# A fused attention and feed-forward kernel: issuing one ScalarE step of the weight preparation one tick later during the first matrix product

## The chip, the core and the metric

The kernel runs on one core of one Trainium2 chip. The metric is the device time of one launch in microseconds (us); lower is better. The core has five engines that run on their own instruction queues, each strictly in order: TensorE (PE) multiplies matrices, VectorE (DVE), ScalarE (ACT) and GpSimd (POOL) work on elements, and SyncE (SP) here only issues DMA transfers. They wait for one another through semaphores.

## The reference

```python
def _attn_ref(q, k, v, g_q, g_k):            # q, k, v: (8, 12, 448, 64) float32
    q_n, k_n = (rmsnorm(q, g_q), rmsnorm(k, g_k))
    scores = np.matmul(q_n, k_n.transpose(0, 1, 3, 2)) / np.sqrt(64)
    attn = softmax(scores)
    return np.matmul(attn, v)

x = attn_out.transpose(0, 2, 1, 3).reshape(3584, 768)
h = x @ w_in                                  # w_in: (768, 2048) float64
g = np.maximum(h, 0.0) ** 2
out = g @ w_out                               # w_out: (2048, 768) float64
```

## The kernel before

**Stages.** The eight batches are taken in four spans of two batches (896 tokens). Span 0 begins with its attention alone. Then comes its first matrix product, called L1 here: `x @ w_in`, relu, square. After that each span's second product (`g @ w_out`) runs interleaved with the next span's attention, and each later span's first product follows. The change concerns L1 of span 0 only, roughly 133 to 261 us of the profiled execution.

**Seven products for eight.** Each matrix product is done by a Strassen-Winograd scheme: a two-by-two block product is made of seven block products, A11, S2, S1, S3, A12, A22 and S4, whose left sides are quadrants of the weights or sums of quadrants. L1 has eight columns of blocks, f = 0 to 7, of seven block products each. Number these products u = 0 to 55, so that u = 7f + position. Within a column the order is A11, S2, S1, S3, A12, A22, S4 (in column 0: A11, S1, A12, S2, S3, S4, A22). Each product is three 128x128 blocks against 448 columns; the trace shows it as six matmuls.

**What follows a product.** The results are collected in PSUM (TensorE's output memory):

- A11: ACT copies it out (`p1`, L1102).
- S2: DVE adds `z = p1 + pb` (L1106).
- S1: DVE adds `y = z + pc` (L1109).
- S3, A22, S4: DVE adds the product to `y` or `z` (L1114), then ACT takes the relu (L1066) and the square (L1068) of the sum.
- A12: ACT takes relu and square straight from PSUM.

Products share banks: `pb`, `pc` and `pd` alternate between two banks. So S3 may start only when S2's add has been made, the next column's S2 only when this column's S4 add has been made, and A22 (which accumulates onto S3's bank) only when S3's add has been made. Each of these three adds has the length of one product, about 2.25 us, between the end of its own product and the start of the product that needs the bank.

**Preparing the weights.** The weights come as float64. Thirty-two chunks n = 0 to 31 (128 partitions x 768 values; 0 to 15 from `w_in`, 16 to 31 from `w_out`) are turned into float32 on the chip, while attention and L1 run. The generator `prepare(t)` does this in four ticks for each t:

- tick 1: SP stores the finished seven blocks of an earlier pair of chunks to DRAM (L598, odd chunks n = t-3 only); DVE clamps the high words of chunk t (L603). The clamp reads what `unsigned(t)` wrote.
- tick 2: ACT scales the low words (L606); DVE shifts bits into a PSUM scratch (L608).
- tick 3: DVE merges sign and bits (L613); DVE adds the parts of chunk t-1 to its float32 value (L579).
- tick 4: POOL forms the sums S1 to S4 for odd chunks (L583; all four operations of a pair run once the chunk's value is there); SP starts loading later words (L543).

`unsigned(n)` is one ACT instruction: the absolute value of the high words of chunk n (Abs, L589, 128x768). It is called for chunk t+1 during `prepare(t)`, and the clamp of chunk t+1 in the next tick waits for it.

**Which tick comes after which product.** The loop over L1 (L1502 to L1507) yields after each product and then runs ticks up to number `min(ALL, EARLY + (ALL - EARLY) * (u - 1) // (N1 - 6))`, that is min(140, 52 + 88(u-1)//50); tick s of chunk t has number 4t + s. So between one and two ticks follow each product. The order of instructions within each engine's queue is the order in which this code emits them; nothing reorders them. Chunks t < 13 are prepared during attention (EARLY // 4 = 13), the rest in L1.

**Loads.** SP loads each weight block (`sw`, five buffers, L672) into the buffer that the product five places earlier has left; the stores of L598 stand in the same queue and wait for POOL's sums.

Of the kernel before, what the change touches and what calls it, by code (L numbers as in the profile page):

```python
# [387 lines left out]
def attention_then_ffn_bounded(  # L388
# [100 lines left out]
    EARLY, ALL = 4 * 13, 4 * (2 * NFC + 3)  # L489
# [9 lines left out]
    def pairs_of(words):  # L499
        both = words.rearrange("p (n two) -> p n two", two=2)  # L500
        return both[:, :, 0], both[:, :, 1]

    def words_of(n):
        place = n % WORDS
        if place == 0:
            at = BLOCKS * 8 * HW + EXPS * NW
            flat = stage[:, at:at + 2 * NW]
        elif place < 3:
            f = (NFC, HF)[place - 1] - 2
            flat = gT[:, f:f + 2, :].rearrange("p f n -> p (f n)")[:, 0:2 * NW]  # L510
        else:
            if (n, "words") not in spare:
                spare[n, "words"] = spare["pool"].tile([P, 2 * NW], F32, tag="words", name="words", bufs=WORDS - 3)
            flat = spare[n, "words"]
        return flat.bitcast(U32)

    def blocks_of(n):
        at = n // 2 % BLOCKS * 8 * HW
        return stage[:, at:at + 8 * HW].rearrange("p (k m) -> p k m", k=8)

    def place_of(n, k):

        return 7 * int(n >= NFC) if k == A21 else k + int(n < NFC)

    def exponents_of(n):
        at = BLOCKS * 8 * HW + n % EXPS * NW
        return stage[:, at:at + NW]
# [17 lines left out]
    def load_words(t, done):  # L545

        while loaded[0] <= t + WORDS - 3 and loaded[0] < max(done, 0) + WORDS:
            load_w(loaded[0])
            loaded[0] += 1

    def prepare(t):

        def there(n):
            return 0 <= n < 2 * NFC

        def parts(n):
            low, high = pairs_of(words_of(n))
            return exponents_of(n), exponents_of(n).bitcast(U32), low, high  # L560

        def value(n, half):
            if not there(n):
                return

            to = ((A11, A12), (A21, A22)) if n < NFC else ((A11, A21), (A12, A22))
            places = [place_of(n, k) for k in to[n % 2]]
            part = slice(half * HW, (half + 1) * HW)
            if not doubles:
                nc.gpsimd.tensor_copy(blocks_of(n)[:, places[half]], words_of(n).bitcast(F32)[:, part])  # L570
                return
            _, eu, low, _ = parts(n)
            if n < EARLY // 4:
                dst = blocks_of(n)[:, places[half]]
                nc.gpsimd.tensor_tensor(*[x.bitcast(I32) for x in (dst, low[:, part], eu[:, part])], ALU.add)
            elif half == 0:
                dst = blocks_of(n)[:, places[0]:places[1] + 1:places[1] - places[0]]
                low, eu = (x.rearrange("p (h m) -> p h m", h=2) for x in (low, eu))
                nc.vector.tensor_tensor(*[x.bitcast(I32) for x in (dst, low, eu)], ALU.add)  # L579

        def total(n, dst, x, y, op):
            if there(n) and n % 2:
                nc.gpsimd.tensor_tensor(*[blocks_of(n)[:, place_of(n, i)] for i in (dst, x, y)], op)  # L583

        def unsigned(n):

            if there(n) and doubles:
                e, _, _, high = parts(n)
                nc.scalar.activation(e, high.bitcast(F32), AF.Abs)  # L589

        if t == 0:
            unsigned(0)
        n = t - 3
        if there(n) and n % 2:
            c = n % NFC // 2
            dst = w1s[c] if n < NFC else w2s[:, c // 4, :, c % 4]
            first = place_of(n, A11)
            nc.sync.dma_start(dst.rearrange("k p m -> p k m"), blocks_of(n)[:, first:first + 7])  # L598
            written[0] = n + 1
        if there(t) and doubles:  # L600
            e, eu, low, high = parts(t)

            nc.vector.tensor_scalar(e, e, 2.0 ** -15, 1.875 * 2.0 ** 16, ALU.max, ALU.min)  # L603
        yield
        if there(t) and doubles:
            nc.scalar.activation(low.bitcast(I32), low, AF.Copy, scale=2.0 ** -29)  # L606
            bits = banks.get("bits", eu)
            nc.vector.tensor_scalar(bits, eu, 3, 0x3FFFFFF8, ALU.logical_shift_left, ALU.bitwise_and)  # L608
        if t < 3:
            load_words(t, t - 1)  # L610
        yield
        if there(t) and doubles:
            nc.vector.scalar_tensor_tensor(eu, high, 0xC0000000, bits, ALU.bitwise_and, ALU.bitwise_or)  # L613
        total(t - 2, S3, A11, A21, ALU.subtract)
        total(t - 2, S4, A12, S2, ALU.subtract)
        value(t - 1, 0)
        if t >= EARLY // 4:
            unsigned(t + 1)
        yield
        if t < EARLY // 4:  # L620
            unsigned(t + 1)
        value(t - 1, 1)
        total(t - 1, S1, A21, A22, ALU.add)
        total(t - 1, S2, S1, A11, ALU.subtract)
        load_words(t, t - 1)
        yield

    def ticks():
        for t in range(2 * NFC + 3):
            yield from prepare(t)  # L630
# [1009 lines left out]
```

## Time and profile before

| | |
|---|---|
| median of 3 runs | 1345.16 us (1345.02 to 1346.12) |
| the profiled execution's own time | 1345.02 us |
| its span, first to last instruction | 1343.1 us |
| TensorE busy | 1324.0 us (99% of the span) |
| VectorE busy | 860.5 us (64%) |
| ScalarE busy | 486.2 us (36%) |
| GpSimd busy | 681.1 us (51%) |
| mean granted TensorE clock | 0.998 |

The profiled execution lasts 1.9 us longer than its span; the difference lies before the first and after the last instruction. A row of the timeline gives the start, the duration, the engine, the line, what is written and read, and in brackets how long the engine had been idle and what released it. On DVE and ACT an instruction can start before the one ahead of it has quite ended, so the distance between two starts is what an instruction costs its queue. A row of the table by stretches gives for each engine its busy time and number of instructions, then the granted clock, the share of the DMA engines' time, and GB/s.

### The profile page before, as it was taken

To read this page: it belongs to the slowest core of one execution; us is meant where nothing else is said; L and a number is where in the kernel's file an instruction comes from. 1 tells how busy PE (TensorE), PEld (TensorE's weight loads), DVE (VectorE), ACT (ScalarE), POOL (GpSimd) and SP (SyncE) were. 2 spreads that over 40 slices of the span, in tenths; PEclk is the share of its full clock that TensorE was granted. 3 is DMA by queue.
4 is the path that set the end of the run, shared out by engine and by line. 5 is a ranking of instruction groups with operands and counts; after the bars stand their busy time and mean duration, and the time that the engine had idled before them with its cause. 6 is when DMAs were issued, how large, how long until landed. Compare 5 with 4: busy or idle time off the path is not lost.

```text
span 1343.1 us, 17769 instructions
## 1 busy us (share of the span) xinstructions
PE 1324.0 (99%) x5930; PEld 699.4 (52%) x5930; DVE 860.5 (64%) x1333; ACT 486.2 (36%) x939; POOL 681.1 (51%) x546
## 2 busy tenths in 40 slices
PE   8999999999999999999999999999999999999997
PEld 3333544444446655444444755444444665556887
DVE  6999888489988233467887523457878723336553
ACT  7886566455541012245543011235554101111000
POOL 5766534376765222647774522448676522322452
PEclk9999999999999999999999999999999999999999
DMA  8978899656664433356656432345664444431333
GB/s 225 240 221 218 289 372 307 213 124 132 133 148 119 102 88 88 97 116 125 145 127 144 109 91 88 95 114 115 134 130 124 120 92 143 128 88 47 115 104 55
DMA packets 413817, 190.18 MB, mean 142 GB/s; under 512 B 282388, under 2 KB 408724, under 8 KB 413716
## 3 DMA queue, kind: packets, MB, share of 16 engines
q1 hardware_dynamic: 406164, 180.21, 51.8%
q0 software_dynamic: 4736, 8.40, 2.4%
q8 instruction: 49, 0.80, 0.3%
q10 hardware_dynamic: 2816, 0.34, 0.2%
q14 instruction: 52, 0.43, 0.1%
HBM read 155.72 MB, written 33.16 MB: 141 GB/s over the span
## 4 chain that ended last, share of the span: by engine, by line
PE 86%; DVE 7%; ACT 3%; DMA 3%; issue 1%; POOL 0%; SPq 0%; DVEq 0%; ACTq 0%; POOLq 0%
PE ps L1198 21%; PE pd L1098 10%; PE pa L1098 10%; PE pc L1098 10%; PE sc L799 7%; PE pav L881 7%; PE pb L1098 5%; PE ps L1381 3%; PE ps L1249 2%; PE pd L1353 2%; PE pc L1353 2%; PE pa L1353 2%; PE pd L1183 1%; PE pc L1183 1%; DMA sw<-w1s 1%
## 5 line engine op out<-in xcount | busy, mean ns | idle before, releaser
L1070 POOL TENSOR_TENSOR gT<-gT 128x448 f32<-128x448 f32 x96 | 93.7, 978 | 258.5 <-ACT gT L1066 258.5
L764 POOL TENSOR_TENSOR half<-half,mhalf 128x28 f32<-128x28 f32 x36 | 185.2, 5145 | 69.5 <-DVE half L763 54.9
L1198 PE MATMUL ps<-gT,sw 128*128 128x448 f32 x432 | 169.3, 545 | 0.0
L1066 ACT ACTIVATE gT<-gT 128x448 f32<-128x448 f32 x96 | 55.4, 577 | 296.2 <-DVE gT L1114 296.2
L1098 PE MATMUL pa<-xT,sw 128*128 128x448 f32 x384 | 154.9, 539 | 0.5 <-DMA sw<-w1s 0.5
L1198 PEld LDWEIGHTS ps<-gT,sw 128*128 128x128 f32 x432 | 80.1, 190 | 87.2 <-issue 85.0
L1198 PE MATMUL ps<-gC,sw 128*128 128x448 f32 x288 | 113.1, 546 | 0.0
L799 PE MATMUL sc<-qkT 64*64 64x448 f32 (+1 forms) x1152 | 110.0, 496 | 0.3 <-ACT pr L801 0.2
L1098 PEld LDWEIGHTS pa<-xT,sw 128*128 128x128 f32 x384 | 72.8, 190 | 71.4 <-issue 71.4
L583 POOL TENSOR_TENSOR gC<-gC 128x384 f32<-128x384 f32 x64 | 76.3, 1209 | 60.2 <-DVE gC L579 58.5
L1114 DVE TENSOR_TENSOR gT<-z,pd 128x448 f32<-128x448 f32 x32 | 19.8, 620 | 102.2 <-PE pd L1098 102.2
L849 POOL DMA_DIRECT2D xT<-factors x72 | 38.0, 532 | 92.8 <-DMA factors<-square 65.7
L1198 PEld LDWEIGHTS ps<-gC,sw 128*128 128x128 f32 x288 | 53.2, 190 | 59.5 <-issue 58.3
L801 ACT ACTIVATE pr<-sc 128x896 f32<-128x896 f32 x87 | 76.9, 908 | 12.3 <-PE sc L799 12.1
L766 POOL TENSOR_TENSOR qk<-qk,half 128x448 f32<-128x448 f32 x72 | 77.1, 1092 | 2.8
L1098 PE MATMUL pd<-xT,sw 128*128 128x448 f32 x192 | 77.9, 542 | 0.2
L1098 PE MATMUL pc<-xT,sw 128*128 128x448 f32 x192 | 77.5, 540 | 0.2 <-DMA sw<-w1s 0.2
L1098 PE MATMUL pd<-xC,sw 128*128 128x448 f32 x192 | 77.4, 539 | 0.0
L1098 PE MATMUL pb<-xC,sw 128*128 128x448 f32 x192 | 77.4, 539 | 0.0
L1098 PE MATMUL pc<-xC,sw 128*128 128x448 f32 x192 | 77.4, 539 | 0.0
L881 PE MATMUL pav<-pr,vt 64*64 64x448 f32 x348 | 72.7, 537 | 0.0
L881 PE MATMUL rest<-pr,vt 64*64 64x448 f32 x348 | 72.7, 537 | 0.0
(282 smaller groups left out, 2453.1 us busy)
## 6 DMA issues: line engine op xcount, KB each, us to landing
sw<-w1s SPq DMA_DIRECT2D x224, 192.0 KB, 2.4
sw<-w2s SPq DMA_DIRECT2D x102, 256.0 KB, 3.4
w1s<-gC SPq DMA_DIRECT2D x8, 1344.0 KB, 6.4
w2s<-gC SPq DMA_DIRECT2D x8, 1344.0 KB, 6.8
qk<-in_q_dram SPq DMA_DIRECT2D x144, 56.0 KB, 2.6
qk<-in_k_dram SPq DMA_DIRECT2D x144, 56.0 KB, 2.4
xT<-factors POOLq DMA_DIRECT2D x72, 112.0 KB, 3.5
words<-in_moe_w_out_dram SPq DMA_DIRECT2D x9, 768.0 KB, 6.9
```

Of the source, the lines that this page charges most:

```text
L583: nc.gpsimd.tensor_tensor(*[blocks_of(n)[:, place_of(n, i)] for i in (dst, x, y)], op)
L764: nc.gpsimd.tensor_tensor(half, half, mhalf, ALU.pow)
L766: nc.gpsimd.tensor_tensor(qkn[:, s], raw[:, s], half[:, s * NG:(s + 1) * NG].rearrange("p g -> p g ()").to_broadcast([P, NG, 32]), ALU.mult)
L799: nc.tensor.matmul(sc[part, h, 0:n], qkT[rows, 0, 1, keys], qkT[rows, 0, 0, of], start=True, stop=True)
L801: nc.scalar.activation(pr, sc[:, :, 0:n], AF.Exp)
L881: nc.tensor.matmul(into, vs[i][rows, h, c, :], probs[i, c][rows, h, :], start=(c == 0), stop=(c == NF), skip_group_check=True)
L1066: nc.scalar.activation(g, src, AF.Relu)
L1070: nc.gpsimd.tensor_tensor(g, g, g, ALU.mult)
L1098: nc.tensor.matmul(ps, stream[n + at][:, c], rhs[:, c], start=first and c == 0, stop=c == HC - 1, skip_group_check=not first)
L1198: nc.tensor.matmul(ps, stream[n][:, c % 4], rhs_of[i][:, c], start=c == 0, stop=c == HF - 1)
L1353: nc.tensor.matmul(ps, lhs[:, c], rhs[:, c], start=first and c == 0, stop=c == HK - 1, skip_group_check=not first)
L1381: nc.tensor.matmul(ps, weights_of(o, m, c // HK)[:, c % HK], rhs_of[i][:, c, part], start=c == 0, stop=c == HF - 1)
```

## The change

In `prepare`, for the chunks that are prepared during L1, the Abs of the next chunk moves from the end of tick 3 to the start of tick 4. For the chunks before, it was there already.

```diff
         value(t - 1, 0)
-        if t >= EARLY // 4:
-            unsigned(t + 1)
         yield
-        if t < EARLY // 4:
-            unsigned(t + 1)
+        unsigned(t + 1)
         value(t - 1, 1)
         total(t - 1, S1, A21, A22, ALU.add)
         total(t - 1, S2, S1, A11, ALU.subtract)
```

No instruction is added or removed, and no other engine's instructions move. Between the two places stands the `yield`: where ticks 3 and 4 follow different products, the ACT instructions that belong to the product in between come ahead of the Abs.

## The prediction

> **What bounds the kernel now.** I read the page first, then L1 by stretches, then the waits inside L1, then the timelines of DVE, ACT, PE, POOL and SP around the moved instruction.
>
> ```profile
> PE 1324.0 (99%) x5930; PEld 699.4 (52%) x5930; DVE 860.5 (64%) x1333; ACT 486.2 (36%) x939; POOL 681.1 (51%) x546
> ```
>
> TensorE has no room in the span as a whole. In L1 it is the same, but DVE is close behind; the columns are PE, PEld, DVE, ACT, POOL, clock, DMA share, GB/s:
>
> ```profile
> 160.00:175.00 15.00, 15.00 (x41) 7.60 (x40) 12.41 (x17) 8.74 (x14) 6.92 (x7) 1.00 1.03 379
> 175.00:190.00 15.00, 14.93 (x40) 7.33 (x39) 13.63 (x17) 9.77 (x15) 5.46 (x6) 1.00 1.00 366
> 190.00:205.00 15.00, 15.00 (x41) 7.60 (x40) 13.56 (x17) 10.64 (x16) 7.41 (x8) 1.00 1.02 372
> ```
>
> A column of seven products lasts 7 x 2.255 = 15.8 us, and of 15 us DVE leaves 1.4 to 2.6 free. Here the reserve ends (DVE, then PE):
>
> ```profile
> 181.91 0.61 DVE L1114 TENSOR_TENSOR gT<-z,pc 128x448 f32<-128x448 f32 x1
> 182.44 1.05 DVE L603 TENSOR_SCALAR gC<-gC 128x768 f32<-128x768 f32 x1
> 183.52 0.96 DVE L608 TENSOR_SCALAR bits<-gC 128x768 uint32<-128x768 uint32 x1
> 184.51 0.95 DVE L613 SCALAR_TENSOR_TENSOR gC<-gC,bits 128x768 uint32<-128x768 uint32 x1
> 185.39 1.72 DVE L579 CUSTOM_DVE_ANT_0 gC<-words,gC 128x1536 uint16<-128x1536 uint16 x1
> 187.03 0.61 DVE L1106 TENSOR_TENSOR z<-p,pb 128x448 f32<-128x448 f32 x1
> ```
>
> ```profile
> 185.20 2.42 PE L1098 MATMUL pc<-xC,sw 128*128 128x448 f32 x6
> 187.69 2.52 PE L1098 MATMUL pd<-xT,sw 128*128 128x448 f32 x6
> 190.05 2.42 PE L1098 MATMUL pa<-xT,sw 128*128 128x448 f32 x6
> 192.30 2.42 PE L1098 MATMUL pd<-xC,sw 128*128 128x448 f32 x6
> ```
>
> S3 of column 3 (u = 24) was due at 185.20 + 2.255 = 187.45; the z add ended at 187.64, S3 started at 187.69, and the product after it 0.34 late. That is DVE's only PE stall in L1. The lateness is never made up: 190.05 to 192.30 is 2.25 again. The clamp took 1.05 instead of its median 0.55, and L579 1.72 instead of 0.95, because POOL's group of four L583 ran from 182.07 to 186.29: each of the two DVE instructions ends 0.37 and 0.82 us after the end of one POOL operation.
>
> **Which Abs really move.** I put the tick formula against the products. Of the chunks t = 13 to 30, ticks 3 and 4 fall after the same product for 8, and for t = 21, 24, 27 only an S2 lies between, which has no ACT instruction: no queue changes. Seven change: t = 13, 25, 28 (past S3's relu and square), 14 (past A22's), 16 (past A12's), 17 and 20 (past S4's). Nothing else moves on ACT, and DVE, POOL, SP and PE keep their orders.
>
> **Price of one move.** The DVE step that pays is the clamp of chunk t+1, which stands right behind (or one product behind) an add whose result ACT must first relu and square. From the rows: add to relu 0.65 (181.91 to 182.55), relu to square 0.61, square to the next 0.49, Abs to clamp 0.93 (160.09 to 161.02): 2.68 after the add's start, against 0.53 before. The clamp comes 2.15 us late, and DVE, in order, makes everything behind it late: bits, merge, value, and the next adds that free banks. Waits for PE on DVE's way give some of it back.
>
> **Chain 1, t = 13 and 14.** The add of S3 (145.38) is followed by clamp 14: 145.91 becomes 148.06. S4's add was waiting for PE until 147.07 and now starts at 148.61 (+1.54). Bits 0.54, 0.58, merge 0.88, value 0.87 follow; A22's add goes from 149.94 to 151.50. Behind it relu, square, Abs 15: clamp 15 goes from 150.57 to 151.50 + 2.67 = 154.17. It falls into POOL's group (now 151.6 to 155.8), so it costs 1.0. Bits 0.99, and column 1's z add goes from 153.91 to 156.18, visible at 156.79. S3 (u = 10) was due at 155.89; it starts at 156.83, with 0.10 for the refill as in the stall shown: **1.04 lost**.
>
> **Chain 2, t = 16.** DVE is 2.2 late, PE 1.04. Clamp 17 now stands behind A12's relu and square as well: 161.02 becomes 164.33, A22's add 162.85 becomes 165.43. Then 0.53, bits 0.99, merge 0.88, value 0.88: S4's add 166.12 becomes 168.73, visible 169.34. The next S2 (u = 15) was due at 167.16 + 1.04 = 168.21: **1.28 lost**. With t = 17, clamp 18 comes at 171.41 and the z add ends at 173.60; S3 is due at 171.67 + 2.32 = 173.99: no loss. By A22's add at 178.64, which had waited 0.95 for PE, DVE is 2.43 late and PE 2.32.
>
> **Chain 3, t = 20.** S4's add 181.91 becomes 184.36, clamp 21 184.36 + 2.67 = 187.03, again in a POOL group (1.0). Bits 0.99 and merge 0.87 bring value to 189.95, the z add to 190.82, visible 191.43. S3 (u = 24) is due at 187.45 + 2.32 = 189.78: 1.80 lost, where 0.34 was lost before: **1.46 more**.
>
> **t = 25 and 28.** Clamp 26 is 2.15 late against PE, but A22's add behind it had waited 1.42 for PE, so 0.75 remains; the z add of u = 36 had ended at 218.54 against S3 at 219.36, 0.82 of room: 0 to 0.14 lost. Behind clamp 29 the waits for PE are 0.92, 0.32, 0.64 and 1.09: nothing lost.
>
> **Sum.** 1.04 + 1.28 + 1.46 + 0.1 = 3.9 us in L1. If a POOL group does not hold up DVE in the new places, the three are 0.6, 0.7 and 0.9, together 2.3. If each hand-over between engines costs 0.04 more, the sum is 5.1; I take 3.9, since these latencies, put through the old order, land within 0.12 us of the old rows.
>
> **Loads.** TensorE also waited for blocks, at 226.44 and 238.48; with the refill that cost 0.42 and 0.73. A later PE could swallow these 1.15. Against that, SP's stores (L598) wait for POOL: 6.9 us in 6 waits in the list of SP's waits. POOL's group for chunk 25 (212.98 to 217.19) comes 0.8 late against PE, the store at 217.21 with it, and the block issued behind it (217.68, 8.7 to landing) is the one that was late at 226.44: up to 0.8 more. Ends -1.15 and +0.8; I take +0.1, since both SP's loads and their use shift with PE.
>
> **After L1** the list of PE's waits has 0.6 us outside L1 and the first attention, so nothing takes the delay back. 1345.02 + 3.9 + 0.1 = 1349.0; the profiled execution stands 0.14 below the median of the three.
>
> A rule that speaks against this: the Trainium skill (Trainium Kernel Development and Optimization, Performance Expectations) calls matmul busy time a bad metric of the distance to roofline and wants LDWEIGHTS busy instead. By it the 52% of PEld would mean that TensorE could catch up a late product, and the sum would be about 0. The rows decide against that: products keep 2.255 us apart after the stall.
>
> **Rivals.** *Not slower:* DVE's own reserve swallows the waits. Its place is the z add of u = 10; it decides if that add comes less than 1.3 us late (its old end 154.52 against S3 at 155.89), where I compute 2.27. For it: 1.4 to 2.6 us free in 15, and PE waits of up to 1.4 on DVE. Against it: the reserve lies before the S4 and A22 adds, and chains 1 and 2 follow one another. Then chain 2 does not start late either, and t = 20 alone leaves at most 1.3: 1345.0 to 1346.3.
>
> *Slower still:* the loads become the wait. The stores for chunks 17 and 25 come 1.0 and 0.8 late against PE and hold up the blocks behind them: 3.9 + 0.8 to 1.8, 1349.7 to 1350.8. For it: DMA share 1.0 until 205. Against it: blocks are issued four products, 9 us, ahead, and landed in 3 to 9.
>
> *Faster by over 0.2%:* the 1.15 of load waits would have to go, all of DVE's waits be covered, and 1.5 more be gained from another order of transfers after L1: below 1342.4. No row speaks for it.
>
> That the change does nothing is excluded only for 11 of 18 chunks by the tick table; for the other seven the order in the code is the order in the queue.
>
> **How the numbers follow.** Forecast 0.65 (own range 1347.3 to 1350.1, from 2.3 and 5.1), loads 0.15, reserve 0.17, faster 0.03, which stands for what no row shows. 0.2% is 2.7 us, about what a measurement of this kernel can tell from no change. All of loads and most of the forecast (0.62) lie beyond it: slower 0.77. Reserve and the forecast's low end: same 0.20. The range reaches from the forecast's low end with the load waits swallowed (2.3 - 1.15: 1346.1) to the high end with loads (5.1 + 0.8: 1350.9).
>
> **What would show it.** In the profile after: clamps L603 idle for ACT L589 in L1, 4 to 7 times up to 2.2 us (before: 0.7 in 2); stalls of 0.6 to 1.8 us ahead of S3 of column 1, S2 of column 2, S3 of column 3, with DVE's add as releaser; L1's last product at 262.7 instead of 258.85. It is wrong if L1 ends within 1 us of before, if the stalls are ahead of other products, or if the time grows outside L1.

## The result, and the profile after

The median of 22 runs is 1347.95 us, against 1345.03 us for 22 runs of the kernel before beside it: 2.92 us more, a ratio of 1.0024 with a 95% interval of 1.0017 to 1.0030. The profiled execution took 1348.41 us (before 1345.02), its span is 1346.5 us (1343.1).

The page's first part. TensorE's busy time is the same (1324.0 before), so the 3.4 us of span are idle time:

```profile
span 1346.5 us, 17769 instructions
PE 1324.1 (98%) x5930; PEld 698.9 (52%) x5930; DVE 862.8 (64%) x1333; ACT 486.2 (36%) x939; POOL 683.5 (51%) x546
```

The list of waits between 145 and 262 us (who waited for whom, us in total, times, longest). VectorE's clamp (L603) waits for ScalarE's Abs (L589) 14.0 us in 8 waits, where before (between 145 and 256 us) it was 0.7 in 2. Three waits of TensorE for VectorE have come in. Before:

```profile
DVE gC L603 <- ACT gC L589: 0.7, 2, 0.3
```

After:

```profile
DVE gC L603 <- ACT gC L589: 14.0, 8, 2.1
...
PE pd L1095 <- DVE z L1103: 1.9, 2, 1.3
...
PE pa L1095 <- DMA sw<-w1s: 1.3, 1, 1.3
...
PE pb L1095 <- DVE gT L1111: 0.8, 1, 0.8
```

TensorE's timeline shows where (L1095 is L1098 of before, three lines up). Starts are 2.255 us apart while nothing is waited for:

```profile
153.44 2.42 PE L1095 MATMUL pc<-xC,sw 128*128 128x448 f32 x6
156.40 2.52 PE L1095 MATMUL pd<-xT,sw 128*128 128x448 f32 x6 [0.54 <-DVE z L1103]
158.76 2.42 PE L1095 MATMUL pa<-xT,sw 128*128 128x448 f32 x6
...
165.52 2.42 PE L1095 MATMUL pa<-xT,sw 128*128 128x448 f32 x6
168.74 2.52 PE L1095 MATMUL pb<-xC,sw 128*128 128x448 f32 x6 [0.80 <-DVE gT L1111]
171.10 2.42 PE L1095 MATMUL pc<-xC,sw 128*128 128x448 f32 x6
...
186.89 2.42 PE L1095 MATMUL pc<-xC,sw 128*128 128x448 f32 x6
190.65 2.52 PE L1095 MATMUL pd<-xT,sw 128*128 128x448 f32 x6 [1.35 <-DVE z L1103]
193.01 2.42 PE L1095 MATMUL pa<-xT,sw 128*128 128x448 f32 x6
...
238.11 2.42 PE L1095 MATMUL pd<-xT,sw 128*128 128x448 f32 x6
241.80 2.49 PE L1095 MATMUL pa<-xT,sw 128*128 128x448 f32 x6 [1.27 <-DMA sw<-w1s]
244.13 2.42 PE L1095 MATMUL pd<-xC,sw 128*128 128x448 f32 x6
```

Take the distance of two starts beyond 2.255, and add what the next distance is too long (the refill). S3 of column 1 loses (2.96 - 2.255) + (2.36 - 2.255) = 0.81; S2 of column 2 loses 1.07; S3 of column 3 loses 1.61; product 46, which waits for its weight block, loses 1.51. Before it was 0.34 at S3 of column 3, 0.42 and 0.73 in waits for blocks at products 41 and 46 (here the two rows of before):

```profile
226.44 2.52 PE L1098 MATMUL pc<-xT,sw 128*128 128x448 f32 x6 [0.15 <-DMA sw<-w1s]
...
238.48 2.49 PE L1098 MATMUL pa<-xT,sw 128*128 128x448 f32 x6 [0.50 <-DMA sw<-w1s]
```

The third stall on VectorE and on ScalarE, against the lines of 181.91 to 187.64 shown of before. The add of S4 is done at 184.20; ScalarE takes relu and square, and only then Abs; the clamp idles 2.05 us, and bits, merge, value and the z add follow it without a gap:

```profile
183.59 0.61 DVE L1111 TENSOR_TENSOR gT<-z,pc 128x448 f32<-128x448 f32 x1
186.25 0.96 DVE L603 TENSOR_SCALAR gC<-gC 128x768 f32<-128x768 f32 x1 [2.05 <-ACT gC L589]
187.25 0.96 DVE L608 TENSOR_SCALAR bits<-gC 128x768 uint32<-128x768 uint32 x1
188.24 0.95 DVE L613 SCALAR_TENSOR_TENSOR gC<-gC,bits 128x768 uint32<-128x768 uint32 x1
189.12 0.95 DVE L579 CUSTOM_DVE_ANT_0 gC<-words,gC 128x1536 uint16<-128x1536 uint16 x1
189.99 0.61 DVE L1103 TENSOR_TENSOR z<-p,pb 128x448 f32<-128x448 f32 x1
```

```profile
184.23 0.58 ACT L1063 ACTIVATE gT<-gT 128x448 f32<-128x448 f32 x1 [1.24 <-DVE gT L1111]
184.84 0.58 ACT L1065 ACTIVATE gT<-gT 128x448 f32<-128x448 f32 x1
185.32 0.89 ACT L589 ACTIVATE gC<-gC 128x768 f32<-128x768 f32 x1
```

L1 lasts from 133.04 to 262.17 by the starts of its first and last product, 129.13 us against 125.62 (133.23 to 258.85): 3.51 more. It starts 0.19 earlier, so its end shifts by 3.3, and the span ends 3.4 later. What comes after L1 takes 1083.1 to 1085.5 us in the eight profiles, longer or shorter without regard to the edit; so the comparison below goes by L1, and that L1's end and the span's end shift alike in this pair is in part luck.

### The profile page after: what moved, and what is told of

It is laid out like the page before. It is cut to its first block, busy times and chain, and to the rows that moved or that the text cites. A ratio compares the mean times of both kernels' runs of the same rounds, so it can differ in the third digit from the quotient of the medians.

```text
span 1346.5 us, 17769 instructions
## 1 busy us (share of the span) xinstructions
PE 1324.1 (98%) x5930; PEld 698.9 (52%) x5930; DVE 862.8 (64%) x1333; ACT 486.2 (36%) x939; POOL 683.5 (51%) x546
## 4 chain that ended last, share of the span: by engine, by line
PE 83%; DVE 8%; ACT 4%; DMA 2%; issue 2%; SPq 1%; POOL 1%; ACTq 0%; DVEq 0%; POOLq 0%
PE ps L1195 19%; PE pd L1095 10%; PE pa L1095 10%; PE pc L1095 9%; PE sc L796 7%; PE pav L878 6%; PE pb L1095 5%; PE ps L1378 3%; PE ps L1246 2%; PE pd L1350 2%; ACT gT L808 2%; PE pc L1350 2%; PE pa L1350 2%; PE pd L1180 1%; PE pc L1180 1%
## 5 line engine op out<-in xcount | busy, mean ns | idle before, releaser
L1095 PE MATMUL pa<-xT,sw 128*128 128x448 f32 x384 | 155.0, 539 | 1.3 <-DMA sw<-w1s 1.3
L1095 PEld LDWEIGHTS pa<-xT,sw 128*128 128x128 f32 x384 | 72.8, 190 | 72.2 <-issue 72.2
L1095 PE MATMUL pd<-xT,sw 128*128 128x448 f32 x192 | 78.0, 542 | 2.1 <-DVE z L1103 1.9
L1095 PE MATMUL pb<-xC,sw 128*128 128x448 f32 x192 | 77.5, 540 | 0.8 <-DVE gT L1111 0.8
L1095 PE MATMUL pc<-xT,sw 128*128 128x448 f32 x192 | 77.4, 539 | 0.0
L1095 PE MATMUL pd<-xC,sw 128*128 128x448 f32 x192 | 77.4, 539 | 0.0
L1095 PE MATMUL pc<-xC,sw 128*128 128x448 f32 x192 | 77.4, 539 | 0.0
```

Source lines behind the costliest of these rows:

```text
L1095: nc.tensor.matmul(ps, stream[n + at][:, c], rhs[:, c], start=first and c == 0, stop=c == HC - 1, skip_group_check=not first)
```

## The experiments

Lost time in L1 by place, refill included, in us; the last column is the distance from the first to the last product's start.

| kernel | S3 col. 1 | S2 col. 2 | S3 col. 3 | block 41 | block 46 | L1 |
|---|---|---|---|---|---|---|
| before | 0 | 0 | 0.34 | 0.42 | 0.73 | 125.62 |
| after | 0.81 | 1.07 | 1.61 | 0 | 1.51 | 129.13 |
| Abs late in 20 only | 0 | 0 | 1.61 | 0 | 1.14 | 126.89 |
| late in all but 13, 14, 20 | 0 | 0.07 | 0.33 | 0 | 1.31 | 125.84 |
| late in 13 and 14 only | 0.82 | 0.35 | 0.34 | 0 | 1.21 | 127.13 |
| after, sums left out | 0.34 | 0.42 | 1.19 | 0 | 1.43 | 127.52 |
| after, loads split | 0.79 | 1.07 | 1.61 | 0 | 0 | 127.61 |
| before, loads split | 0 | 0 | 0.33 | 0 | 0 | 124.46 |

The times alone are too coarse to tell one theory from another where they differ by under 1 us: each 95% interval below spans about 2.4 us. There the rows of one profile per kernel decide.

Two theories stood against the chain of VectorE's waits: that every move costs its share, and that the time is lost in waits for weight blocks.

**One move: chunk 20.** Edit, on the kernel before:

```diff
-        if t >= EARLY // 4:
+        if t >= EARLY // 4 and not (t == 20):
             unsigned(t + 1)
         yield
-        if t < EARLY // 4:
+        if t < EARLY // 4 or t == 20:
             unsigned(t + 1)
```

> The Abs of the next chunk goes to tick 4 only in chunk t = 20; all others stay in tick 3. Chain theory (the Abs stands behind relu and square, VectorE's clamp waits about 2.1 us for it, and a late add holds a PSUM bank): one stall grows, ahead of S3 of column 3, from 0.34 to about 1.6 us with the refill; nothing ahead of S3 of column 1 and S2 of column 2. Load waits near products 41 and 46 as before (0.42 and 0.73). Time about 1.3 us above before. Rival of equal shares (each of the seven moves costs a seventh of the 2.9 us): 0.4 us. Rival of the loads (the time is lost in waits for weight blocks): S3 of column 3 as before, more wait at products 41 or 46.

Measured: ratio 1.0010 (1.0001 to 1.0019), medians 1345.95 against 1344.88; the interval covers the 0.4 us of equal shares too. Only the stall ahead of S3 of column 3 grew, to the size that it has in the changed kernel:

```profile
188.91 2.52 PE L1098 MATMUL pd<-xT,sw 128*128 128x448 f32 x6 [1.35 <-DVE z L1106]
```

L1 is 1.27 longer. This one move makes 1.27 us, three times an equal share; the waits for blocks sum to 1.14, as before to 1.15, but all at product 46.

**Four real moves and eleven empty ones.** The same edit with the condition

```diff
+        if t >= EARLY // 4 and not (t not in (13, 14, 20)):
```

> The Abs goes to tick 4 in all chunks from 13 to 30 but 13, 14 and 20: four of the seven real moves (16, 17, 25, 28) and the eleven that change no queue. Chain theory: the clamps still wait for Abs, three times about 2 us and once about 1 more than before, but the waits fit in VectorE's reserve when chunks 13 and 14 do not come before: S4's add of column 1 ends by about 167.0 against S2's due start at 167.16, no stall ahead of columns 1 and 2, 0.34 at column 3 as before; time within 0.3 us of before. Rival of equal shares: 4/7 of 2.9, 1.7 us. Rival of the loads: the store for chunk 25 is still late, 0.8 us more at products 41 or 46.

Measured: ratio 0.9999 (0.9990 to 1.0008). The 1.7 us of equal shares would be 1.0013. The clamps do wait, 8.3 us in 5 waits, one of 0.33 being there before too, but TensorE hardly notices. VectorE and TensorE in column 1 and 2 (VectorE's rows, then TensorE's):

```profile
162.01 0.69 DVE L603 TENSOR_SCALAR gC<-gC 128x768 f32<-128x768 f32 x1 [1.89 <-ACT gC L589]
...
165.88 0.61 DVE L1114 TENSOR_TENSOR gT<-z,pc 128x448 f32<-128x448 f32 x1
168.53 0.56 DVE L603 TENSOR_SCALAR gC<-gC 128x768 f32<-128x768 f32 x1 [2.04 <-ACT gC L589]
```

```profile
164.32 2.42 PE L1098 MATMUL pa<-xT,sw 128*128 128x448 f32 x6
166.58 2.49 PE L1098 MATMUL pb<-xC,sw 128*128 128x448 f32 x6
```

S4's add is visible at 165.88 + 0.61 = 166.49, and S2 is due at 164.32 + 2.255 = 166.58: it fits by 0.09. So about 8 us of waiting on VectorE cost TensorE 0.07 us at the products, and equal shares fall. (L1 is 0.22 longer; product 46 waits 1.31 in all, against 1.15 for both blocks before.)

**The first two moves.** The same edit with the condition

```diff
+        if t >= EARLY // 4 and not (t in (13, 14)):
```

> The Abs goes to tick 4 only in chunks 13 and 14. Chain theory: 0.8 us ahead of S3 of column 1 as in the changed kernel, and since VectorE is then still late, about 0.3 ahead of S2 of column 2 (where the changed kernel loses 1.07); column 3 as before. Time about 1.1 us above before. Rival of equal shares: 0.8 us, half of it at each. Rival of the loads: no stall at columns 1 and 2.

Measured: ratio 1.0011 (1.0002 to 1.0021), which cannot tell 1.1 us from 0.8. The two stalls are there, 0.82 and 0.35:

```profile
156.00 2.52 PE L1098 MATMUL pd<-xT,sw 128*128 128x448 f32 x6 [0.55 <-DVE z L1106]
...
167.62 2.52 PE L1098 MATMUL pb<-xC,sw 128*128 128x448 f32 x6
```

L1 is 1.51 longer, 0.4 more than expected: product 18 lost 0.30 as well (2.48 us after the one before, the next 2.33 after it), which the list of waits gives to no releaser, and the wait at product 46 was 1.21. The block of product 18 is issued behind a store that left at 166.24 (165.00 in the kernel before, whose L1 began 0.6 later); that this store is the cause was not tried.

The three runs together: column 2 loses 0.35 from chunks 13 and 14 alone, 0.07 from 16 and 17 alone, and 1.07 from all four. The moves of columns 1 and 2 add to one another because the second falls on a VectorE that is still late from the first. Column 3 does not: it loses 1.61 with chunk 20 alone and 1.61 with all seven.

**GpSimd's share.** Edit, on the kernel after; it leaves out the sums S1 to S4 of four chunks:

```diff
-            if there(n) and n % 2:
+            if there(n) and n % 2 and n not in (13, 15, 17, 19):
```

> The changed kernel, with GpSimd's sums S1 to S4 left out for chunks 13, 15, 17 and 19, so that the weights made from these chunks are not the reference's. Theory that GpSimd's sums hold up the late clamps: clamps 15, 17 and 21 take 0.55 us instead of 0.96, 1.22 and 0.96; the stalls ahead of S3 of column 1, S2 of column 2 and S3 of column 3 fall from 0.81, 1.07 and 1.61 to about 0.4, 0.5 and 1.2. Rival (the waits for Abs alone make the stalls): clamps and stalls as in the changed kernel.

Measured (one execution, 1346.48 us, so no ratio): the stalls are 0.34, 0.42 and 1.19. VectorE ahead of the third:

```profile
185.02 0.56 DVE L603 TENSOR_SCALAR gC<-gC 128x768 f32<-128x768 f32 x1 [2.03 <-ACT gC L589]
```

Clamps 15, 17 and 21 took 0.56 each instead of 0.96, 1.22 and 0.96. So of the 3.49 us of VectorE's stalls 1.54 come about because the late clamps fall beside GpSimd's sums, and 1.95 from the waits for Abs alone. The Trainium skill (SBUF — State Buffer, Who interferes with whom) says that a VectorE instruction in a 2-port mode, which tensor_scalar can enter, and a GpSimd instruction contend for one port pair: whoever issues first has it for the whole instruction, and the other blocks. The rows agree: the clamp, a tensor_scalar, takes 0.4 to 0.66 us more, less than one GpSimd operation (median 1.01). That the port pair is the reason was not tried apart from leaving the sums out.

**The loads, in both kernels.** Edit:

```diff
-                if u == 5 * N1 // 7:
+                if u == 5 * N1 // 7 - 3:
                     load_v(NAT)
+                if u == 5 * N1 // 7 + 2:
                     load(NAT + 2)
```

> The changed kernel, with the loads of the next v issued after product 37 and those of the third pair's q and k after product 42, instead of all ten after product 40. Theory: the wait ahead of product 46 (1.51 us in the changed kernel) is set by SyncE's queue, where ten issues of 7 us stand between the block of product 44 and that of product 45, and then a store stands ahead of the block of product 46; with the loads split, block 46 is issued 3 us earlier and the wait goes; at product 41 up to 0.4 may come back. VectorE's three stalls stay at 0.8, 1.1 and 1.6. Time 1.0 to 1.5 us below the changed kernel, so about 1.5 to 2 above the kernel before. Rival (DMA bandwidth sets the wait, the total moved by then is the same): product 46 still waits over 1 us.

> The kernel before, with the same split of the loads. Theory: the wait ahead of product 46 (0.73 us) goes, that at product 41 (0.42) stays or grows a little; VectorE's one stall of 0.34 stays; time 0.3 to 0.8 us below before. If both hold, the two kernels then differ by VectorE's three stalls alone, 0.81 + 1.07 + 1.61 - 0.34 = 3.15 us up to the end of the first product. Rival (bandwidth): as the kernel before.

Measured: after with loads split 1.0019 (1.0010 to 1.0028), before with loads split 0.9990 (0.9981 to 0.9999), medians 1347.42 and 1344.62 against 1345.31. In both, no wait for a block is left in L1. The first was expected 1.5 to 2 us above the kernel before; the medians are 2.11 apart, with an interval of 1.3 to 3.8, so the time neither bears that out nor refutes it. SyncE's queue, first in the kernel after, then with the loads split:

```profile
234.48 0.42 SPq L669 DMA_DIRECT2D sw<-w1s  x1
235.01 0.38 SPq L598 DMA_DIRECT2D w2s<-gC  x1
235.48 3.83 SPq L669 DMA_DIRECT2D sw<-w1s  x4
```

```profile
229.92 0.37 SPq L598 DMA_DIRECT2D w2s<-gC  x1
231.16 0.32 SPq L669 DMA_DIRECT2D sw<-w1s  x1
231.53 3.90 SPq L688 DMA_DIRECT2D qk<-in_q_dram  x4
```

The loads are twelve issues, not ten as the expectation has it: four of v, four each of q and k. With the eight of q and k behind it and the four of v earlier, the block of product 46 is issued at 231.16 instead of 235.48, 4.32 us earlier, and the 1.51 are gone. So its place in SyncE's queue sets this wait. That bandwidth has no part in it is not shown: in the changed kernel the block took 6.18 us from its issue to its landing, against a median of 2.4 on the page, and the split puts the transfers of q and k behind it too.

Without waits for blocks, L1 of the two kernels is 127.61 and 124.46: 3.15 us apart, and their own stalls differ by 0.79 + 1.07 + 1.61 - 0.33 = 3.14. The medians of the two are 2.80 apart. The split loads in the kernel before are 0.1% faster than it, at the edge of what the runs can tell. One part was missed: at product 41 the wait was expected to stay or come back, and it went. That wait shows in the profile of the kernel before and in none of the seven others, so it may belong to that one execution.

## Why the prediction was right, point by point

- **Which Abs move.** Right: after the change seven clamps wait longer than before, those of the seven moves named, and the eleven empty ones together with 16, 17, 25 and 28 gave a ratio of 0.9999. For the eleven the tick table shows that nothing moves; the prediction's sentence on this, "is excluded only for 11 of 18", has it the wrong way round.
- **Price of one move.** Right: 2.68 us were computed from the add's start to the clamp's, and it is 2.65 to 2.67 (183.59 to 186.25, for one); the idle time ahead of these clamps is 2.04 to 2.06 (1.36 past A12).
- **Chains 1, 2 and 3.** The places were right, the sizes each 0.2 us too large: 1.04, 1.28 and 1.80 were computed, 0.81, 1.07 and 1.61 measured. In chain 1 the mis-sized term is the distance on VectorE from clamp and bits to an add: I took 0.55 and 0.99. Before an add it is 0.48 and 0.87, as these rows of the kernel after show, and the kernel before shows the 0.87 too (173.57 to 174.44):

```profile
147.86 0.56 DVE L603 TENSOR_SCALAR gC<-gC 128x768 f32<-128x768 f32 x1 [2.04 <-ACT gC L589]
148.34 0.61 DVE L1111 TENSOR_TENSOR gT<-z,pc 128x448 f32<-128x448 f32 x1
...
154.86 0.96 DVE L608 TENSOR_SCALAR bits<-gC 128x768 uint32<-128x768 uint32 x1
155.73 0.61 DVE L1103 TENSOR_TENSOR z<-p,pb 128x448 f32<-128x448 f32 x1
```

With these the same sum gives 0.81. Chain 2 took the lateness over from chain 1, and with it a distance of 1.05 (157.29 to 158.34) in which S3's add had waited for its product; behind a late VectorE it is 0.87 (159.11 to 159.98). With both put right the sum gives 1.08. Chain 3 does not start from the others at all: A22's add of column 2 starts at 180.32, 0.03 after its product's end (177.87 + 2.42), so VectorE is no later than TensorE there, where I had it 0.13 later (2.45 against 2.32). And 187.03 + 1.0 + 0.99 + 0.87 is 189.89, not 189.95. Without these two the sum gives 1.61, what chunk 20 alone makes as well. Net, VectorE's part is 3.15, not 3.8.
- **t = 25 and 28.** Right: no stall; 0.1 was kept for it and is not there.
- **GpSimd in the new places.** 2.3 us was the sum without it, by 0.6, 0.7 and 0.9 (the last beyond the old 0.34). The run without the sums gave 0.34, 0.42 and 1.19, the last 0.85 beyond the old 0.34: smaller by 0.26, 0.28 and 0.05. The first two hold the same mis-sized distances.
- **Loads.** +0.1 was taken, between -1.15 and +0.8; it was 1.51 - 1.15 = +0.36. The mechanism that I gave for the upper end, a late store ahead of block 41, did not show: product 41 did not wait. The wait sits at product 46 and follows SyncE's twelve issues, which took 6.98 us (227.40 to 234.38) instead of 6.62. Of the lower end, swallowed waits, only the 0.42 at product 41 came, and the wait at 46 grew by 0.78.
- **After L1.** Nothing is made up inside L1: after each stall the products are 2.255 apart again, and the busy time is unchanged. As I read the rule on LDWEIGHTS busy that was weighed, they would have caught up; the section speaks of the distance to roofline, not of that, and names MFU beside LDWEIGHTS busy. Past L1 the shift of 3.3 is 3.4 at the span's end, but what follows L1 scatters by 2.4 us over the profiles, so that one pair cannot show it to a tenth.
- **Rivals.** Reserve: it swallows chunks 16, 17, 25 and 28 as long as 13 and 14 stay, as the second run shows, but not 13 and 14 together (neither was tried alone), and not 20. It hung on the z add ahead of product 10 coming less than 1.3 us late; it came 2.01 late (155.73 against 153.91, with L1 begun 0.19 earlier). Loads: one tenth of the loss in the profiled execution, 0.36 of 3.39.

The sum of 4.0 against 3.39 in the profiled execution and 2.92 between the medians is thus the right chain with terms that were 0.2 us too long three times and 0.1 for t = 25 and 28 that did not come; against them a wait for a block was sized 0.26 too small, and sat at another product than the one named.

## What to carry to other kernels

An instruction that is moved within its own queue cost here what the queue of its reader lost, and only from the point where that queue's next deadline was missed. So list, for each reader, what stands behind it and how much room the first bank to be freed has; four moves with about 8 us of waits were almost free here, and one move with 2 us cost 1.27. Waits added up only where the second fell on a queue that was still late from the first; look for the idle time that resets it.

## What the runs showed of the hardware that was not expected

What a VectorE instruction costs its queue depended on what followed it. In L1 of all eight profiles, from 145 us on, the L608 of 0.96 us held a merge, which reads its result, for 0.98 to 1.00, and an add, which does not, for 0.86 to 0.88 where the add had no product to wait for; the clamp of 0.55 held the L608 that reads it for 0.58 to 0.60, and such an add for 0.48 to 0.50. That the reading makes the difference, and not the kind of the instruction that follows, was not tried. One distance of each kind in chain 1 was worth 0.2 us there, and was carried on into chain 2.
